# One of three shifted copies of each VectorE score group made on GpSimd, in two forms, in a fused attention and token-MLP kernel

## The chip, the cores and the metric

The kernel runs on one core of a Trainium2 chip. The metric is device time in microseconds, the median of its runs. The profile shows five engines: PE (TensorE), ACT (ScalarE), DVE (VectorE), POOL (GpSimd) and SP (SyncE, which here issues the DMAs). Each works through its own queue in order, and they wait for one another by semaphores.

## What is computed

Cut to what matters (x is 2048 rows of 640 bf16 values, 32 heads of 20, and F = 1536):

```python
xn = layernorm(x)
qkv = xn @ wqkv                                   # 640 x 1920
scores = einsum("bhqd,bhkd->bhqk", q, k) * 20**-0.5
o = einsum("bhqk,bhkd->bhqd", softmax(scores), v)
s = o.transpose(0, 2, 1, 3).reshape(B, S, D) @ wo
u = gelu(einsum("bsd,sf->bdf", layernorm(xn), w1) + b1)
y = einsum("bdf,fs->bds", u, w2) + b2
out = x + s * silu(y.transpose(0, 2, 1))
```

## The kernel before

**Tiles.** Heads are taken four at a time (a group G, with the heads g = 0 to 3 in four 32-row strips of TensorE), queries 512 at a time (p). A pair (G, p) is a pass, 32 in all. In a pass, keys come in 16 chunks of 128, so a pass has 64 score tiles of 128 keys by 512 queries, each made by one matmul (`emit_st`, L1206) into one of the eight PSUM banks.

**Two ways to an exponential.** Most score tiles are exponentiated on ScalarE (`emit_exp`, L1235), two or three banks at a time, into `pt_sb`. The others go to VectorE in groups of four, the four heads of one chunk, called a quad below. VectorE makes the exponential by the bits of bf16: the scores are already scaled so that one unit is 1/128 of a power of two, and adding a constant and storing the sum as an unsigned 16-bit integer gives the bits of a rough exponential. `emit_op1` (L1246) does that straight from PSUM: one instruction a tile, called an eviction below. To smooth the error of the rough curve, `emit_top` (L1268) then makes three copies of the whole quad (2048 elements a partition), shifted by 32, 64 and 96 (`DK`). TensorE multiplies all four versions with `v`, the shifted ones with copies of `v` that are scaled accordingly (`vs_sb`, factors `AK`), and sums them in one PSUM bank (`pv_mm`, L1284). ScalarE's tiles need one such matmul, VectorE's four. Chunks that may go to VectorE are those in `RC`, five of sixteen in a pass.

**Buffers.** `dt_sb` has eight tiles (`NTILE`) of one quad version each; a free list `tfree` hands them out. A quad takes one tile for its evictions and one for each copy, and gives them back when TensorE has read them. At most three quads live at once (`NLIVE`). The two groups of three banks that ScalarE works from (`ACT_GROUPS`) alternate; the last bank of a group can be lent to VectorE (`lent`), and a further bank (`JB`) is shared with the projection and MLP work. A bank whose tile VectorE has evicted is given to the next score matmul, which waits for that eviction.

**What sets the order.** The program is written by a planner that runs when the kernel is built. `Prog` keeps a clock for each engine; every task has a booked cost; `ready` gives the earliest start by the tasks that it depends on. The loop at the end of `schedule` picks the engine that can start first and the candidate of lowest priority number. `pe_cands` and `eng_cands` list the candidates, `OPTS` and `PLAN` change the planner's options every 16 score tiles (`WIN`), and `loads` and `dve_load` estimate what work is left. The finished order stands in the engines' queues; at run time it is fixed, and only semaphores delay it. The rest of the work (projections, MLP matmuls, their evictions and products, the softmax denominators in `ep_steps` with L1400 to L1411, the output) is cut into steps that the planner fits between the score tiles.

**Around the change.** After the fourth eviction of a quad, `emit_op1` puts it on `dtop`. `emit_top` makes copies k = 1, 2, 3 in turn, each a task of VectorE booked at `dv(2048, .26)`. `d["fin"][k]` holds the planned end of version k, which the PV candidate in `pe_cands` uses; versions are multiplied in order of k, some early and the rest later (`PARTS`). With k = 3 the quad leaves `dtop`. GpSimd does small things only: constants and memsets in the lead-in (L503 to L513), the powers of the layer norms (L545, L566), the memset of `wqk_sb` (L1565) and two residual additions in the tail (L1609).

Of the kernel before, what the change touches and what calls it, by code (L numbers as in the profile page):

```python
# [6 lines left out]
dt = mybir.dt  # L7
ALU = mybir.AluOpType
# [31 lines left out]
class Prog:  # L40
# [7 lines left out]
    def __init__(self, nc, n_lanes=8):  # L48
        self.nc = nc
        self.n_lanes = n_lanes  # L50
        self.cengs = list(self.COMPUTE) + [f"d{i}" for i in range(n_lanes)]
        self.cidx_of = {c: i for i, c in enumerate(self.cengs)}
        self.tasks = {e: [] for e in self.COMPUTE}
        self.ctasks = {c: [] for c in self.cengs}
        self.gcount = 0
        self.lane_rr = 0
        self.known = {e: [0] * len(self.cengs) for e in self.COMPUTE}
        self.T = {e: 0.0 for e in self.COMPUTE}
        self.busy = {e: 0.0 for e in self.COMPUTE}
        self.pipe = 0.0  # L60
        self.pe_end = 0.0
        self.low = 0
        self.lowt = 0.0
        self.alog = []

    def lat(self, eng, src):
        return 0.0 if src == eng else self.LAT[eng] + (40.0 if eng == "act" and src == "pe" else 45.0 if eng == "dve" and src == "pe" else 0.0)
# [15 lines left out]
                    r = max(r, t.fin + self.lat(eng, t.ceng))  # L83
        return r

    def _add(self, eng, ceng, fn, reads, writes, name, extra_req=(), cost=100.0, tail=None):
        t = _Task(eng, ceng, fn, name)
        t.gidx = self.gcount
        self.gcount += 1
        self.tasks[eng].append(t)  # L90
        self.ctasks[ceng].append(t)
        t.cidx = len(self.ctasks[ceng])
        req = {}

        def need(tt):
            if tt is None:
                return
            if eng == "pe" and tt.ceng == "pe":
                return
            cur = req.get(tt.ceng)  # L100
            if cur is None or tt.cidx > cur.cidx:
                req[tt.ceng] = tt

        for s in reads:
            assert s.w is not None, f"read of uninit slot {s.name} by {name}"
            need(s.w)
        for s in writes:
            need(s.w)
            for r in s.readers.values():
                if r is not t:  # L110
                    need(r)
        for tt in extra_req:
            need(tt)
        start = self.T[eng]
        for tt in req.values():
            start = max(start, tt.fin + self.lat(eng, tt.ceng))
        kn = list(self.known[eng])
        for tt in sorted(req.values(), key=lambda x: -x.gidx):
            ci = self.cidx_of[tt.ceng]
            if kn[ci] >= tt.cidx:  # L120
                continue
            t.waits[tt.ceng] = tt
            if tt.ceng in self.COMPUTE:
                tt.need_inc = True
            klg = tt.klg
            for i in range(len(kn)):
                if klg[i] > kn[i]:
                    kn[i] = klg[i]
        self.known[eng] = list(kn)
        kn[self.cidx_of[ceng]] = max(kn[self.cidx_of[ceng]], t.cidx)  # L130
        t.klg = kn
        for s in reads:
            s.readers[ceng] = t
        for s in writes:
            s.w = t
            s.readers = {}
        t.t0 = start
        if ceng not in self.COMPUTE:
            start = max(start, 700.0)
            if tail is not None:  # L140
                self.T[eng] = start + cost
                self.pipe = max(self.pipe, start) + cost
                t.fin = self.pipe - cost + tail
            else:
                self.T[eng] = start + 450.0
                self.pipe = max(self.pipe, start + 600.0) + cost
# [27 lines left out]
    def dve(self, fn, reads=(), writes=(), name="dve", cost=300.0):  # L174
        return self._add("dve", "dve", fn, reads, writes, name, cost=cost)

    def pool(self, fn, reads=(), writes=(), name="pool", cost=500.0):
        return self._add("pool", "pool", fn, reads, writes, name, cost=cost)
# [82 lines left out]
class _Kern:  # L261
# [75 lines left out]
        "00000100100010", "10020100100010", "30000100100010", "00002000001000", "01012000000000", "00000000000000",  # L337
        "00000320000000", "00022310000000", "00022311000000",
    )
    PARTS = (2,)  # L340
    DX = (1, 2, 3)
    V1A, V1B = 0.8, 4.0
# [15 lines left out]
    def build(self):  # L358
# [4 lines left out]
        with es:  # L363
# [30 lines left out]
            sb("b1h_sb", [P, FC], f32)  # L394
            sb("b2h_sb", [P, NB], f32)
            sb("bload_sb", [P, FC + NB], bf)
            t["ps_all"] = E(nc.psum_tensor("ps_all", [P, 4096], f32))
            t["qk_dram"] = nc.dram_tensor("qk_scratch_dram", [2, 560, S], bf)
            t["oT_dram"] = nc.dram_tensor("oT_scratch_dram", [8 * P, S], bf)
# [16 lines left out]
    def schedule(self):  # L416
# [80 lines left out]
        def small(fn):  # L497
            def f(e):
# [5 lines left out]
        pr.pool(lambda e: e.memset(cst_sb[:, 1:2], 1.0), writes=[S_("csc")], name="csc0", cost=60)  # L504
        pr.pool(lambda e: e.memset(cst_sb[0:64, 1:2], self.LOG2E * 128.0 / math.sqrt(float(DH))), reads=[S_("csc")],
                writes=[S_("csc")], name="csc1", cost=60)
        pr.pool(lambda e: e.memset(idb_sb[:], 0.0), writes=[S_("idb")], name="id0", cost=200)
        pr.pool(lambda e: e.affine_select(idb_sb[:], idb_sb[:], pattern=[[-1, P]], compare_op=ALU.not_equal, fill=1.0,
                                          base=0, channel_multiplier=1), reads=[S_("idb")], writes=[S_("idb")],
# [551 lines left out]
        dop1 = []  # L1061
        lent = set()
        dtop = []
        pv_pass = [0]
        pv_tot = [UP] * NP
        pv_left = [UP]
# [103 lines left out]
        def d_take(g, bk):  # L1170
            d = d_cur[0]
            if d is None:
                q, c, r = d_claimable()
                claimed.add((q, c))
                dlive[0] += 1
                d = d_cur[0] = dict(q=q, c=c, r=r, todo=[0, 1, 2, 3], tl=[tfree.pop(0), None, None, None], fin=[0.0] * 4, left=4, pk=0)
# [12 lines left out]
            return u  # L1189
# [52 lines left out]
        def emit_op1():  # L1242
            d, g, bk = dop1.pop(0)
            w = dt_sb[:, d["tl"][0], g, :]
            src = ps(bk)
            tk = pr.dve(lambda e: e.tensor_scalar(w, src, WOFF, 0.0, ALU.add, ALU.max), reads=[bank_slot[bk]],  # L1246
                   writes=[S_(f"dt{d['tl'][0]}_{g}")], name=f"dw{d['q']}_{d['c']}_{g}", cost=601.0)
# [12 lines left out]

        def emit_top():
# [5 lines left out]
            dk = float(self.DK[k])  # L1267
            tk = pr.dve(lambda e: e.tensor_scalar(dst, src, dk, None, ALU.add),  # L1268
                        reads=[S_(f"dt{b0}_{g}") for g in range(4)], writes=[S_(f"dt{b}_{g}") for g in range(4)],
                        name=f"dT{d['q']}_{d['c']}_{k}", cost=dv(2048, .26))  # L1270
            dtop[0][1] += 1
            d["fin"][k] = tk.fin
            if k == 3:
                dtop.pop(0)
                if not self.EARLY:
                    dquads.append((tk.fin, d))
                if d["pk"] > 0:
                    tfree.append(b0)

        def pv_mm(q, g, lhsT, rhs, reads, cost, name, last):  # L1280
            k = pv_seen.get((q, g), 0)
# [31 lines left out]
        def emit_pv(items, quads):  # L1313
# [6 lines left out]
            for d, n_ in quads:  # L1320
                for k in range(d["pk"], d["pk"] + n_):
                    for g in range(4):
                        seq.append(("d", d, k, g))
                    if k > 0 or d["tl"][3] is not None:
# [340 lines left out]
        def pe_cands(T):  # L1665
# [27 lines left out]
            if acc_ok[0] and pv_pass[0] < NP:  # L1693
# [28 lines left out]
                okp = bool(pick) and (min(cnt) >= 1 or len(pick) == rem or (tail and len(mine)))  # L1722
                if quads:
                    d0 = quads[0][1]
                    have = sum(f > 0.0 for f in d0["fin"])
# [104 lines left out]
        def dve_load(T):  # L1830
            x = max(0.0, pr.T["dve"] - T) + 602.0 * len(dop1)
            for d, k in dtop:
                x += 600.0 * (4 - k)
            return x

        def do_st(grp, us):
# [52 lines left out]
        def eng_cands(eng, T):  # L1889
# [11 lines left out]
            if eng == "dve":  # L1901
# [3 lines left out]
                if dtop and tfree:  # L1905
                    d, k = dtop[0]
                    b0, b = d["tl"][0], tfree[0]
                    c.append((self.TOPP, pr.ready("dve", [S_(f"dt{b0}_{g}") for g in range(4)],
                                             [S_(f"dt{b}_{g}") for g in range(4)]), emit_top))
            return c  # L1910

        def loads():
# [7 lines left out]
            live += [x[0] for x in dop1] + [x[0] for x in dtop]  # L1920
            for x in {id(x): x for x in live}.values():
                pe += 216.0 * (4 - x["pk"])
                d += 597.0 * sum(f == 0.0 for f in x["fin"][1:])
            return a - done_cost["act"], pe - done_cost["pe"], d - done_cost["dve"]

        self.loads = loads
# [85 lines left out]
```

The softmax here doesn't subtract the row's maximum and nothing guards it: scores larger than these inputs give would overflow.

## Time and profile before

| | |
|---|---|
| median of 2 runs | 755.69 us (755.53 to 755.85) |
| profiled execution, span | 753.7 us |
| ACT busy | 729.9 us (97%), 695 instructions |
| DVE busy | 721.0 us (96%), 1320 instructions |
| PE busy | 717.6 us (95%), 10302 instructions |
| POOL busy | 15.6 us (2%), 22 instructions |
| exponentials, L1235 | 672, 710.5 us |
| evictions, L1246 | 496, 328.2 us |
| shifted copies, L1268 | 372, 241.9 us, median 689 ns each |
| granted TensorE clock | 1.000 |

The span runs from the first to the last instruction of one profiled execution; the median of the runs is 2.0 us longer. Busy time counts an engine's own instructions, not what it issues or waits for. Consecutive instructions of an engine overlap a little, so 372 copies of 687 ns on average count 241.9 us. In the groups of instructions, the figures after the bar are busy time, the mean length of one, and the idle time of the engine just before the group with what ended it.

### The profile page before, as it was taken

Reading aid. Unit: us, or ns where it says so; the run is one execution under the profiler, and the core shown is the slowest. Engines: PE = TensorE matmul, PEld = TensorE weight load, DVE = VectorE, ACT = ScalarE, POOL = GpSimd, SP = SyncE. Lnnn points to the kernel's source line nnn. Section 1 sums busy time; section 2 is a strip of 40 time slices with the busy share of each in tenths; the row PEclk is TensorE's granted clock in tenths of the full one; section 3 lists DMA queues with packets and bytes.
Section 4 is the critical chain, followed back from the end, with each engine's and each line's share of the span. In section 5 each row is a group of like instructions: output and inputs, shape, how many; then the busy total and the mean of one; then the engine's idle time right before and its main releaser. Section 6 shows DMA issues by size and latency. Waiting matters only on the chain.

```text
span 753.7 us, 23158 instructions
## 1 busy us (share of the span) xinstructions
PE 717.6 (95%) x10302; PEld 240.7 (32%) x10302; DVE 721.0 (96%) x1320; ACT 729.9 (97%) x695; POOL 15.6 (2%) x22
## 2 busy tenths in 40 slices
PE   9999999999999999999999999999999988998997
PEld 7432223222323232323223323233333232222222
DVE  8869999999999999999999999999999999999997
ACT  4999999999999999999999999999999999999993
POOL 4200000000000000000000000000000000000001
PEclk9999999999999999999999999999999999999999
DMA  9584111110313031121014022223124340011011
GB/s 245 109 167 57 38 26 38 20 36 7 86 14 77 13 68 38 35 61 21 7 37 111 26 49 52 47 54 102 44 57 82 76 150 11 6 47 48 13 47 36
DMA packets 117143, 42.54 MB, mean 56 GB/s; under 512 B 75300, under 2 KB 115876, under 8 KB 116996
## 3 DMA queue, kind: packets, MB, share of 16 engines
q1 hardware_dynamic: 117044, 41.07, 23.9%
q8 instruction: 80, 1.31, 0.7%
q14 instruction: 19, 0.16, 0.1%
HBM read 26.37 MB, written 10.22 MB: 49 GB/s over the span
## 4 chain that ended last, share of the span: by engine, by line
ACT 85%; PE 12%; DVE 2%; DMA 1%; issue 0%; POOL 0%
ACT pt_sb L1235 83%; PE ps_all L1284 4%; PE ps_all L644 4%; PE ps_all L1206 4%; ACT zt_sb L840 1%; ACT zt_sb L835 1%; PE ps_all L929 1%; DMA xnT_sb<-regC 1%; DVE bst_sb L531 0%; DVE bst_sb L533 0%; DMA regA<-in_A_x_dram 0%; DVE regC L549 0%; DVE regC L1607 0%; PE ps_all L683 0%; DVE xnT_sb L611 0%
## 5 line engine op out<-in xcount | busy, mean ns | idle before, releaser
L1235 ACT ACTIVATE pt_sb<-ps_all 128x1024 bf16<-128x1024 f32 (+1 forms) x672 | 710.5, 1226 | 2.4 <-PE ps_all L1206 1.9
L1246 DVE TENSOR_SCALAR dt_sb<-ps_all 128x512 uint16<-128x512 f32 x496 | 328.2, 684 | 10.1 <-PE ps_all L1206 8.3
L1206 PE MATMUL ps_all<-qk_sb 32*128 32x512 bf16 x2048 | 266.7, 384 | 27.7 <-ACT pt_sb L1235 24.8
L1268 DVE TENSOR_SCALAR dt_sb<-dt_sb 128x2048 uint16<-128x2048 uint16 x372 | 241.9, 687 | 1.4
L1206 PEld LDWEIGHTS ps_all<-qk_sb 32*128 32x128 bf16 x2048 | 67.0, 91 | 283.8 <-ACT pt_sb L1235 231.8
L1284 PE MATMUL ps_all<-dt_sb,vs_sb 128*21 128x512 bf16 x1488 | 124.6, 382 | 0.8 <-DVE dt_sb L1268 0.7
L1284 PE MATMUL ps_all<-pt_sb,v_sb 128*21 128x512 bf16 x1552 | 124.2, 382 | 0.9 <-DVE tr_sb L1400 0.6
L644 PE MATMUL ps_all<-regB,regA 128*32 128x128 bf16 (+1 forms) x1536 | 68.2, 301 | 0.7 <-DVE regB L845 0.3
L644 PE MATMUL ps_all<-regC,regA 128*32 128x512 bf16 (+1 forms) x1536 | 68.4, 301 | 0.0
L1284 PE MATMUL ps_all<-dt_sb,v_sb 128*21 128x512 bf16 x496 | 49.0, 384 | 0.3 <-DVE tr_sb L1400 0.2
L644 PE MATMUL ps_all<-xnT_sb,wqk_sb 128*32 128x512 bf16 x640 | 48.2, 382 | 0.3 <-DVE zt_sb L814 0.2
L1284 PEld LDWEIGHTS ps_all<-dt_sb,vs_sb 128*21 128x21 bf16 x1488 | 31.5, 91 | 41.3 <-issue 21.9
L1284 PEld LDWEIGHTS ps_all<-pt_sb,v_sb 128*21 128x21 bf16 x1552 | 28.7, 90 | 47.7 <-issue 38.0
L644 PEld LDWEIGHTS ps_all<-regB,regA 128*32 128x32 bf16 x1536 | 27.2, 96 | 27.0 <-issue 13.1
L644 PEld LDWEIGHTS ps_all<-regC,regA 128*32 128x32 bf16 x1536 | 27.3, 96 | 25.6 <-issue 13.4
L929 PE MATMUL ps_all<-wv_sb,xnT_sb 128*128 128x128 bf16 (+3 forms) x160 | 29.5, 302 | 0.1
L644 PE MATMUL ps_all<-wv_sb,xnT_sb 128*32 128x480 bf16 x320 | 23.0, 369 | 0.0
L1400 DVE STREAM_TRANSPOSE tr_sb<-ps_all 128x512 f32<-128x512 f32 x31 | 22.1, 711 | 0.9 <-PE ps_all L1284 0.7
L644 PEld LDWEIGHTS ps_all<-xnT_sb,wqk_sb 128*32 128x32 bf16 x640 | 13.7, 95 | 18.2 <-issue 7.7
L1284 PEld LDWEIGHTS ps_all<-dt_sb,v_sb 128*21 128x21 bf16 x496 | 12.6, 90 | 21.3 <-issue 14.7
L814 DVE TENSOR_SCALAR zt_sb<-ps_all,b2h_sb 128x512 bf16<-128x512 f32 (+1 forms) x32 | 17.2, 544 | 0.0
L1044 DVE CAST v_sb<-ps_all 128x480 bf16<-128x480 f32 (+1 forms) x22 | 13.4, 610 | 3.3 <-PE ps_all L737 3.1
(82 smaller groups left out, 307.0 us busy)
## 6 DMA issues: line engine op xcount, KB each, us to landing
regA<-in_B_w_dram SPq DMA_DIRECT2D x6, 1024.0 KB
regA<-in_B_w_dram SPq DMA_DIRECT2D x8, 768.0 KB
qk_sb<-qk_scratch_dram SPq DMA_DIRECT2D x56, 80.0 KB
qk_scratch_dram<-qs_sb SPq DMA_DIRECT2D x32, 128.0 KB
regA<-in_A_x_dram SPq DMA_DIRECT2D x6, 640.0 KB
ok_scratch_dram<-on_sb SPq DMA_DIRECT2D x96, 20.0 KB
out_dram<-regC SPq DMA_DIRECT2D x3, 640.0 KB
wqk_sb<-in_A_wqkv_dram SPq DMA_DIRECT2D x2, 480.0 KB
```

What stands on the lines that cost most here:

```text
L644: fns.append(lambda e, c=c, e_=e_: e.matmul(oc(c, e_), lhsT[:, c:e_], rhs, start=start, stop=stop, tile_position=(0, c)))
L814: steps.append(("dve", lambda e, z=z, i=i, jj=jj: e.tensor_scalar(z[:, c0:c0 + n], ps(bk, n, i * n), 0.5, bias[:, jj:jj + 1], ALU.mult, AL ...
L835: steps.append(("act", lambda e: e.activation(tt_, tt_, AF.Tanh, scale=1.5957691216), [stt], [stt], f"th{j}", ac(n)))
L840: steps.append(("act", lambda e: e.activation(tt_, z, AF.Tanh), sz, [stt], f"th2_{j}", ac(n)))
L929: steps.append(("pe", lambda e, c=c, k=k: e.matmul(ap, oT_sb[0:k, c, b * 128:(b + 1) * 128], wo_ap[0:k, c, c0:c0 + n], start=(opens and c ...
L1044: return lambda e: e.tensor_copy(dst, src)
L1206: pr.pe(lambda e, outp=outp, lhsT=lhsT, rhs=rhs, g=g: e.matmul(outp, lhsT, rhs, start=True, stop=True, tile_position=(32 * g, 0)), reads=[ ...
L1235: tk = pr.act(lambda e: e.activation(outp, inp, AF.Exp, scale=math.log(2.0) / 128.0), reads=[bank_slot[b] for b in banks[:n]], writes=[S_( ...
L1246: tk = pr.dve(lambda e: e.tensor_scalar(w, src, WOFF, 0.0, ALU.add, ALU.max), reads=[bank_slot[bk]], writes=[S_(f"dt{d['tl'][0]}_{g}")], n ...
L1268: tk = pr.dve(lambda e: e.tensor_scalar(dst, src, dk, None, ALU.add), reads=[S_(f"dt{b0}_{g}") for g in range(4)], writes=[S_(f"dt{b}_{g}" ...
L1284: pr.pe(lambda e: e.matmul(outp, lhsT, rhs, start=(k == 0), stop=last, tile_position=(0, 32 * g)), reads=reads, writes=[bank_slot[AB]], na ...
L1400: steps.append(("dve", lambda e: e.transpose(tr_sb[:, :], ps(AB)), [bank_slot[AB]], [S_("tr")], f"epT{q}", 632.0))
```

## The change

The third copy (k = 3) of each quad moves from VectorE to GpSimd. Quads are numbered; an even one is made as before, an immediate added to 2048 two-byte integers, and an odd one as 1024 32-bit integers, each of which holds two neighbours, to which a 32-bit constant with 96 in both halves is added (`sh_sb`, broadcast along the row). A quad's GpSimd task may be planned as soon as its four evictions are, independent of the two VectorE copies. The planner books 2000 ns (`GCOST`) for either form. A new clock pair `port` makes the planner place VectorE's copies and GpSimd's additions so that they do not overlap in its plan; it puts no wait into the program and holds for no other operation. The estimates of VectorE's remaining work count two copies a quad in place of three. `PLAN` is as it was.

```diff
+        self.port = {"dve": 0.0, "pool": 0.0}
...
+        if lock:
+            start = max(start, self.port["pool" if eng == "dve" else "dve"])
+            self.port[eng] = start + cost
...
+    GCOST = 2000.0
...
+            sb("sh_sb", [P, 4], dt.int32)
...
+        sh16 = t["sh_sb"][:, 0:1].bitcast(u16)
+        pr.pool(lambda e: e.memset(sh16, float(self.DK[3])), writes=[S_("shc")], name="shc", cost=60)
...
             if d["left"] == 0:
                 dtop.append([d, 1])
+                ptop.append(d)
...
-                        name=f"dT{d['q']}_{d['c']}_{k}", cost=dv(2048, .26))
+                        name=f"dT{d['q']}_{d['c']}_{k}", cost=dv(2048, .26), lock=True)
...
-            if k == 3:
+            if k == 2:
                 dtop.pop(0)
+            issued(d)
...
+        def emit_ptop():
+            d = ptop.pop(0)
+            b0, b = d["tl"][0], tfree.pop(0)
+            d["tl"][3] = b
+            src = dt_sb[:, b0, :, :]
+            dst = dt_sb[:, b, :, :]
+            if d["n"] % 2:
+                i32 = dt.int32
+                s32 = bass.AP(dt_sb, b0 * 2048, [[self.NTILE * 2048, P], [1, 2048]]).bitcast(i32)
+                d32 = bass.AP(dt_sb, b * 2048, [[self.NTILE * 2048, P], [1, 2048]]).bitcast(i32)
+                c32 = bass.AP(t["sh_sb"], 0, [[4, P], [0, 1024]])
+                fn = lambda e: e.tensor_tensor(d32, s32, c32, ALU.add)
+            else:
+                dk = float(self.DK[3])
+                fn = lambda e: e.tensor_scalar(dst, src, dk, None, ALU.add)
+            tk = pr.pool(fn, reads=[S_(f"dt{b0}_{g}") for g in range(4)] + [S_("shc")],
+                         writes=[S_(f"dt{b}_{g}") for g in range(4)], name=f"dP{d['q']}_{d['c']}_3", cost=self.GCOST,
+                         lock=True)
+            d["fin"][3] = tk.fin
+            issued(d)
...
+            if eng == "pool" and ptop and tfree:
+                b0, b = ptop[0]["tl"][0], tfree[0]
+                c.append((30.0, max(pr.port["dve"], pr.ready("pool", [S_(f"dt{b0}_{g}") for g in range(4)],
+                                                             [S_(f"dt{b}_{g}") for g in range(4)])), emit_ptop))
```

Since the copies of a quad can now end out of turn, `prefix(d)` counts how many versions are done in order of k, and the PV candidate uses that count; `issued(d)` returns the first tile once all three copies have been planned.

More of the change, by code (lines that the diff above doesn't have):

```diff
@@ L84, in ready, with _add @@
         return r
-    def _add(self, eng, ceng, fn, reads, writes, name, extra_req=(), cost=100.0, tail=None):
+    def _add(self, eng, ceng, fn, reads, writes, name, extra_req=(), cost=100.0, tail=None, lock=False):
         t = _Task(eng, ceng, fn, name)
@@ L172, in act, with dve, pool @@
         return self._add("act", "act", fn, reads, writes, name, cost=cost)
[L174 to L178, printed above, removed]
+    def dve(self, fn, reads=(), writes=(), name="dve", cost=300.0, lock=False):
+        return self._add("dve", "dve", fn, reads, writes, name, cost=cost, lock=lock)
+    def pool(self, fn, reads=(), writes=(), name="pool", cost=500.0, lock=False):
+        return self._add("pool", "pool", fn, reads, writes, name, cost=cost, lock=lock)
     def dma(self, fn, reads=(), writes=(), name="dma", lane=None, cost=3000.0, over=(), tail=None):
@@ L1063, in schedule @@
         dtop = []
+        ptop = []
         pv_pass = [0]
@@ L1175, in d_take @@
                 dlive[0] += 1
-                d = d_cur[0] = dict(q=q, c=c, r=r, todo=[0, 1, 2, 3], tl=[tfree.pop(0), None, None, None], fin=[0.0] * 4, left=4, pk=0)
+                d = d_cur[0] = dict(q=q, c=c, r=r, todo=[0, 1, 2, 3], tl=[tfree.pop(0), None, None, None], fin=[0.0] * 4, left=4, pk=0, iss=0, n=stats["dve_units"] // 4)
                 stats["dve_units"] += 4
@@ L1269, in emit_top, with issued, prefix @@
                         reads=[S_(f"dt{b0}_{g}") for g in range(4)], writes=[S_(f"dt{b}_{g}") for g in range(4)],
-                        name=f"dT{d['q']}_{d['c']}_{k}", cost=dv(2048, .26))
+                        name=f"dT{d['q']}_{d['c']}_{k}", cost=dv(2048, .26), lock=True)
             dtop[0][1] += 1
             d["fin"][k] = tk.fin
-            if k == 3:
+            if k == 2:
                 dtop.pop(0)
+            issued(d)
[19 more added lines that the diff above has]
+            issued(d)
+        def issued(d):
+            d["iss"] += 1
+            if d["iss"] == 3:
                 if not self.EARLY:
-                    dquads.append((tk.fin, d))
+                    dquads.append((max(d["fin"]), d))
                 if d["pk"] > 0:
-                    tfree.append(b0)
+                    tfree.append(d["tl"][0])
+        def prefix(d):
+            n = 0
+            while n < 4 and d["fin"][n] > 0.0:
+                n += 1
+            return n
         def pv_mm(q, g, lhsT, rhs, reads, cost, name, last):
@@ L1323, in emit_pv @@
                         seq.append(("d", d, k, g))
-                    if k > 0 or d["tl"][3] is not None:
+                    if k > 0 or d["iss"] == 3:
                         freed.append(d["tl"][k])
@@ L1724, in pe_cands @@
                     d0 = quads[0][1]
-                    have = sum(f > 0.0 for f in d0["fin"])
+                    have = prefix(d0)
                     left = have - d0["pk"]
@@ L1832, in dve_load @@
             for d, k in dtop:
-                x += 600.0 * (4 - k)
+                x += 600.0 * (3 - k)
             return x
@@ L1907, in eng_cands @@
                     b0, b = d["tl"][0], tfree[0]
-                    c.append((self.TOPP, pr.ready("dve", [S_(f"dt{b0}_{g}") for g in range(4)],
-                                             [S_(f"dt{b}_{g}") for g in range(4)]), emit_top))
+                    c.append((self.TOPP, max(pr.port["pool"], pr.ready("dve", [S_(f"dt{b0}_{g}") for g in range(4)],
+                                             [S_(f"dt{b}_{g}") for g in range(4)])), emit_top))
+            if eng == "pool" and ptop and tfree:
+                b0, b = ptop[0]["tl"][0], tfree[0]
+                c.append((30.0, max(pr.port["dve"], pr.ready("pool", [S_(f"dt{b0}_{g}") for g in range(4)],
+                                                             [S_(f"dt{b}_{g}") for g in range(4)])), emit_ptop))
             return c
@@ L1922, in loads @@
                 pe += 216.0 * (4 - x["pk"])
-                d += 597.0 * sum(f == 0.0 for f in x["fin"][1:])
+                d += 597.0 * sum(f == 0.0 for f in x["fin"][1:3])
             return a - done_cost["act"], pe - done_cost["pe"], d - done_cost["dve"]
```

## The prediction

> **What bounds the kernel now.** I read the busy table first, then the cost groups of ScalarE and VectorE, then the busy time by stretch.
>
> ```profile
> span 753.7 us, 23158 instructions
> PE 717.6 (95%) x10302; PEld 240.7 (32%) x10302; DVE 721.0 (96%) x1320; ACT 729.9 (97%) x695; POOL 15.6 (2%) x22
> ```
>
> Three engines stand within 12 us of each other, so the shares alone do not say which one sets the end. The idle time in front of the groups does:
>
> ```profile
> L1235 ACT ACTIVATE pt_sb<-ps_all 128x1024 bf16<-128x1024 f32 (+1 forms) x672 | 710.5, 1226 | 2.4 <-PE ps_all L1206 1.9
> L1246 DVE TENSOR_SCALAR dt_sb<-ps_all 128x512 uint16<-128x512 f32 x496 | 328.2, 684 | 10.1 <-PE ps_all L1206 8.3
> L1206 PE MATMUL ps_all<-qk_sb 32*128 32x512 bf16 x2048 | 266.7, 384 | 27.7 <-ACT pt_sb L1235 24.8
> L1268 DVE TENSOR_SCALAR dt_sb<-dt_sb 128x2048 uint16<-128x2048 uint16 x372 | 241.9, 687 | 1.4
> ```
>
> The 672 exponentials wait 2.4 us in all, while the score matmuls wait 24.8 us for them: ScalarE is the bound, TensorE follows it, and VectorE runs level with it. The stretches show where ScalarE idles at all (columns after the length: PE, PEld, DVE, ACT, POOL busy):
>
> ```profile
> 20.00:40.00 20.00, 17.95 (x188) 7.89 (x188) 16.77 (x59) 20.00 (x16) 4.52 (x4) 1.00 0.64 132
> 40.00:120.00 80.00, 76.36 (x978) 22.98 (x982) 73.56 (x131) 79.18 (x77) 0.00 (x0) 1.00 0.34 60
> ...
> 300.00:400.00 100.00, 97.02 (x1500) 30.61 (x1497) 97.36 (x168) 99.78 (x98) 0.00 (x0) 1.00 0.15 32
> 400.00:500.00 100.00, 96.50 (x1617) 32.22 (x1614) 97.60 (x171) 100.00 (x98) 0.00 (x0) 1.00 0.26 62
> ...
> 740.00:754.00 14.00, 9.92 (x78) 3.60 (x77) 8.06 (x19) 1.76 (x2) 2.26 (x2) 1.00 0.13 47
> ```
>
> From 40 to 740 us ScalarE is busy 698.5 of 700 us. Everything else it idles lies in the lead-in and the tail, which the change hardly touches.
>
> **What it removes.** 124 of the 372 VectorE copies, at 241.9/372 = 0.65 us of busy time each: 80.6 us. VectorE's sum falls from 721.0 to 640.4 us. What stands in the order of the built program decides what this is worth: 672 exponentials before and after, 496 evictions before and after. The planner gives VectorE no more score tiles, so ScalarE keeps its 729.9 us, and the freed VectorE time can buy back at most the 2.4 us ahead of the exponentials. I take -1 us.
>
> **What it adds, and its price.** 124 GpSimd additions, alternately 2048 two-byte elements with an immediate and 1024 words with a tensor of constants. The trace has neither; its rows of GpSimd bound both:
>
> ```profile
> L1609 POOL TENSOR_TENSOR regC<-regC,regA 128x512 bf16<-128x512 bf16 x2 | 2.3, 1148 | 237.8 <-DVE regC L1607 237.8
> ...
> L511 POOL MEMSET wp_sb<- 128x1280 bf16 x1 | 1.2, 1164 | 0.0
> ...
> L508 POOL TENSOR_SCALAR_AFFINE_SELECT idb_sb<-idb_sb 128x128 bf16<-128x128 bf16 x1 | 0.3, 292 | 0.2 <-POOL idb_sb L507 0.2
> ...
> L1633 POOL MEMSET idb_sb<- 128x128 bf16 x1 | 0.2, 204 | 0.0
> ```
>
> The two memsets give (1164-204)/1152 = 0.83 ns an element over a fixed 0.10 us. The two-input addition is (1148-97)/512 = 2.05 ns an element; the select, with one input and an index pattern, (292-97)/128 = 1.5 ns. The packed form is that two-input addition on 1024 words: 0.10 + 2.10 = 2.2 us (a pure write of 1024 elements would give 0.95 us). The two-byte form lies between a memset's 1.8 us and the select's 3.2 us; since it has the read but no pattern, I take 2.0 us, near the memset. The planner itself books 2.0 us for either, and its bookings for the rows above (1200 and 1180 ns) are close to them. GpSimd's sum is then 62 x 2.0 + 62 x 2.2 = 260 us; GpSimd itself is no bound. Only the 32-bit form's constant row is read besides; its one small memset at the start costs about 0.1 us under the loads.
>
> The Trainium skill's page "GPSIMD Engine Reference", section 3.1, puts two-input work at about 2.5 cycles an element and the best simple loop at 1.8 cycles, at 1.2 GHz: by that an estimate of 2.1 us for the packed form, as the row says, but 3.1 us for the two-byte one, which would lead to the slow rival's sum below instead of mine.
>
> **The wait it adds.** Whether a VectorE copy can run beside a GpSimd instruction is seen once in the lead-in, as a hint:
>
> ```profile
> 2.75 2.83 POOL L513 MEMSET v_sb<- 128x1024 bf16 x1
> ```
> ```profile
> 5.30 0.31 DVE L542 TENSOR_SCALAR st_sb<-st_sb 128x2 f32<-128x2 f32 x1
> ...
> 6.91 0.17 DVE L542 TENSOR_SCALAR st_sb<-st_sb 128x2 f32<-128x2 f32 x1
> ```
>
> A tiny SBUF-to-SBUF operation that started under the memset took 0.31 us in place of 0.17 and ended at 5.61, just after the memset at 5.58. So I count a VectorE SBUF-to-SBUF operation as standing still until GpSimd's instruction ends, and the reverse. The lower bound is no blocking at all.
>
> The Trainium skill says the same as a rule and against this change ("SBUF — State Buffer", section "Who interferes with whom"): VectorE's fast two-port modes and GpSimd hold one port pair by an exclusive lock, for the whole instruction. By the rule every overlapping copy waits to the end; by the single row alone the size of the effect on a 2048-element copy stays open.
>
> Now the order. In 56 of the 124 quads a VectorE copy directly follows the fourth eviction, so VectorE goes first and GpSimd waits 0.65 us. I then walked VectorE's order from the point where the GpSimd addition can start to the next SBUF-to-SBUF operation, adding the rows' durations; what the addition outlasts this cover by is blocking, if VectorE never idles. Its median is about 1.9 us, mostly three evictions. Summed over 124: 37 us for additions of 1.8 us, 52 for 2.0, 69 for 2.2, 170 for 3.2. At my prices (52+69)/2 = 60 us; with the two-byte form at 3.2 us, (170+69)/2 = 120 us; bounds 0 to 120. VectorE's sum becomes 640.4 + 60 = 700 us, still under 721. So VectorE does not become the bound, but it gets lumpy: behind a blocked copy stand the next evictions (L1246), for which the score matmul that refills that bank waits, two groups later, and behind it the whole TensorE queue and ScalarE.
>
> Of the 60 us, 38 arise at the shifted copies alone, which the planner's new lock already spaces; the other 22 us come from operations that it does not lock (softmax scaling L1411, GELU products, the vs copies). A third of those 22 us should get past the roughly 0.7 us that a bank has in hand: +7 us (0 to 22).
>
> **The third copy is late.** It took 0.65 us right behind two others; now it takes 2.0 to 2.2 us plus up to one VectorE copy in front. For 33 of the 124 the order leaves only one to three ScalarE instructions (1.06 us each: 710.5/672) between its issue and the PV matmul that reads it. Behind that matmul in TensorE's queue stands the next score group. At 0.15 us each: +5 us (0 to 25, the latter where half of them run 1.2 us over).
>
> **The tail.** The last quad's copies were three at 0.65 us; two of them and a GpSimd addition, one behind the other, are 3.4 us: +1.4 us at most. Output-projection matmuls and two later exponentials cover some of it; I take +0.5 (0 to 2.5). SP's and ScalarE's queues keep their instructions, and no DMA is added. GpSimd's own queue now holds the wqk memset (L1565) and the two last additions (L1609) among or behind the copies; nothing else waits for them before the tail, and the memset, which waits for TensorE, stands in the order between two copies, where it can hold back one of them once.
>
> **The sum.** The profiled execution spans 753.7 us; the median of the runs, 755.69, is 2.0 above. 753.7 - 1 + 7 + 5 + 0.5 = 765.2, plus 2.0: 767.2, rounded to 767 us.
>
> **The rivals.**
> *Slower: the two-byte addition runs like the select.* 3.2 us for half of the additions and 120 us of blocking put VectorE at 760 us; with the 13.3 us that it idles in the first 40 and last 14 us that is 774 span, 776 time, and late third copies bring up to 25 us more: 776 to 801, 788 as its middle. For it: the select is the only one-input row. Against: its pattern. It decides once blocking passes 753.7 - 13.3 - 640.4 = 100 us, on the line from 60 at 2.0 us to 120 at 3.2 us: at about 2.8 us for the two-byte form.
> *Hidden.* Blocking is small or falls into VectorE's 80.6 us of new idle time, and PV comes late anyway: 754 to 757. For it: 27.7 us of TensorE waits ahead of the score matmuls. Against: ScalarE has no idle time in which a stall could vanish.
> *Faster by more than 2%*: ScalarE's instructions would have to fall by 15 us, and the order says that they do not. Nearly excluded; 740.
>
> **How the numbers follow.** 2% (740.6 to 770.8) is about what a measurement of this kernel can tell from no change. The forecast (757 to 776) gets 0.45, with 0.10 of it above 770.8; hidden 0.15; the slow rival 0.38, with 0.03 of it below 770.8; faster 0.02. So slower 0.45, within 2% 0.53, faster 0.02. The range runs from the hidden case to the middle of the slow one and somewhat beyond: 755 to 792.
>
> **What would show it.** Right: 672 exponentials at 710 us; idle time ahead of them of 8 to 20 us, put down to score matmuls; the copies' mean above 687 ns by waiting; GpSimd forms near 2.0 and 2.2 us. Wrong: a two-byte form of 2.8 us or more (slow rival), copies that keep 687 ns (hidden), or fewer exponentials.

## The result, and the profile after

The changed kernel takes 1008.64 us (median of 2 runs, 1008.55 to 1008.73) where the kernel before takes 755.69: 1.3345 times as long, with an interval of 1.3306 to 1.3383. Slower by 253 us, far outside the range that was forecast. First the head of its profile:

```profile
span 1006.6 us, 23129 instructions
...
PE 828.6 (82%) x10282; PEld 254.6 (25%) x10282; DVE 861.5 (86%) x1196; ACT 752.0 (75%) x695; POOL 494.1 (49%) x147
```

GpSimd is busy 494 us, not 260 + 16. VectorE, which gave away 124 copies, is busy 140 us longer than before. ScalarE, the bound before, is busy for 75% of the span in place of 97%. The groups say why:

```profile
L1244 ACT ACTIVATE pt_sb<-ps_all 128x1024 bf16<-128x1024 f32 (+1 forms) x672 | 731.3, 1166 | 229.0 <-PE ps_all L1215 220.5
L1301 POOL TENSOR_SCALAR dt_sb<-dt_sb 128x2048 uint16<-128x2048 uint16 x62 | 345.8, 5578 | 282.5 <-DVE dt_sb L1255 275.7
L1255 DVE TENSOR_SCALAR dt_sb<-ps_all 128x512 uint16<-128x512 f32 x496 | 329.0, 681 | 85.9 <-PE ps_all L1215 84.1
L1215 PE MATMUL ps_all<-qk_sb 32*128 32x512 bf16 x2048 | 304.7, 424 | 61.9 <-DVE dt_sb L1255 46.5
L1278 DVE TENSOR_SCALAR dt_sb<-dt_sb 128x2048 uint16<-128x2048 uint16 x248 | 318.6, 1303 | 2.6 <-PE ps_all L1326 1.3
L1298 POOL TENSOR_TENSOR dt_sb<-dt_sb,sh_sb 128x1024 int32<-128x1024 int32 x62 | 132.7, 2141 | 188.6 <-DVE dt_sb L1255 173.9
```

The two-byte addition takes 5.58 us, 2.8 times the forecast; the packed one 2.14, as forecast. VectorE's remaining copies last 1303 ns on average in place of 687, at the same instruction and shape. ScalarE sits idle 229 us ahead of the 672 exponentials, whose number did not change, 220.5 of it for score matmuls; before, it was 2.4. So 227 of the 253 us lie in that number. Most of the rest is busy time of the same exponentials, 731.3 in place of 710.5 us: their mean length fell, but fewer of them follow one another without a pause, and so they overlap less. One piece of the timeline shows the whole chain (start, length in us, engine, line; in brackets the idle time before and its releaser):

```profile
510.70 5.37 POOL L1301 TENSOR_SCALAR dt_sb<-dt_sb 128x2048 uint16<-128x2048 uint16 x1 [3.04 <-DVE dt_sb L1255]
...
512.56 4.05 DVE L1278 TENSOR_SCALAR dt_sb<-dt_sb 128x2048 uint16<-128x2048 uint16 x1
...
516.53 1.27 DVE L1255 TENSOR_SCALAR dt_sb<-ps_all 128x512 uint16<-128x512 f32 x2
517.26 0.60 PE L1215 MATMUL ps_all<-qk_sb 32*128 32x512 bf16 x1 [2.90 <-DVE dt_sb L1255]
...
517.90 1.45 ACT L1244 ACTIVATE pt_sb<-ps_all 128x1536 bf16<-128x1536 f32 x1 [3.07 <-PE ps_all L1215]
```

GpSimd's two-byte addition runs from 510.70 to 516.07. A VectorE copy that is issued at 512.56 ends at 516.61, 0.54 us after GpSimd: it has stood still until GpSimd was done, and most of its usual 0.69 us came after that. The next evictions stand behind it in VectorE's queue and run from 516.53. A score matmul needs the bank that the first of them empties, and has by then held up TensorE for 2.90 us; ScalarE, which needs the scores, sits idle for 3.07. A good part of VectorE's busy time in this profile is therefore time in which it stands blocked: waiting for GpSimd counts as the length of the instruction, not as idle time in front of it. Idle time alone would not have shown this.

### The profile page after: what moved, and what is told of

It reads as the page before. It is cut to its first block, busy times and chain, and to the rows that moved or that the text cites. A ratio compares the mean times of both kernels' runs of the same rounds, so it can differ in the third digit from the quotient of the medians.

```text
span 1006.6 us, 23129 instructions
## 1 busy us (share of the span) xinstructions
PE 828.6 (82%) x10282; PEld 254.6 (25%) x10282; DVE 861.5 (86%) x1196; ACT 752.0 (75%) x695; POOL 494.1 (49%) x147
## 4 chain that ended last, share of the span: by engine, by line
PE 46%; DVE 43%; ACT 7%; issue 2%; DMA 0%; DVEq 0%; SPq 0%
DVE dt_sb L1278 20%; PE ps_all L1326 16%; PE ps_all L1215 15%; PE ps_all L652 13%; DVE dt_sb L1255 11%; ACT pt_sb L1244 7%; PE ps_all L937 2%; DVE on_sb L1453 2%; DVE zt_sb L851 1%; DVE tr_sb L1442 1%; DVE zt_sb L822 1%; DVE regC L962 1%; DVE regC L952 1%; DVE zt_sb L837 1%; DVE qs_sb L1055 1%
## 5 line engine op out<-in xcount | busy, mean ns | idle before, releaser
L1244 ACT ACTIVATE pt_sb<-ps_all 128x1024 bf16<-128x1024 f32 (+1 forms) x672 | 731.3, 1166 | 229.0 <-PE ps_all L1215 220.5
L1301 POOL TENSOR_SCALAR dt_sb<-dt_sb 128x2048 uint16<-128x2048 uint16 x62 | 345.8, 5578 | 282.5 <-DVE dt_sb L1255 275.7
L1215 PE MATMUL ps_all<-qk_sb 32*128 32x512 bf16 x2048 | 304.7, 424 | 61.9 <-DVE dt_sb L1255 46.5
L1278 DVE TENSOR_SCALAR dt_sb<-dt_sb 128x2048 uint16<-128x2048 uint16 x248 | 318.6, 1303 | 2.6 <-PE ps_all L1326 1.3
L1298 POOL TENSOR_TENSOR dt_sb<-dt_sb,sh_sb 128x1024 int32<-128x1024 int32 x62 | 132.7, 2141 | 188.6 <-DVE dt_sb L1255 173.9
L1326 PE MATMUL ps_all<-dt_sb,vs_sb 128*21 128x512 bf16 x1488 | 141.3, 434 | 88.1 <-DVE dt_sb L1278 88.0
L1326 PE MATMUL ps_all<-pt_sb,v_sb 128*21 128x512 bf16 x1552 | 137.1, 419 | 0.7 <-ACT pt_sb L1244 0.2
L652 PE MATMUL ps_all<-regB,regA 128*32 128x128 bf16 (+1 forms) x1536 | 78.2, 335 | 4.6 <-DVE zt_sb L822 4.5
L652 PE MATMUL ps_all<-xnT_sb,wqk_sb 128*32 128x512 bf16 x640 | 55.7, 430 | 4.9 <-DVE dt_sb L1255 3.1
L1453 DVE TENSOR_TENSOR on_sb<-tr_sb,rden_sb 128x320 bf16<-128x320 f32 x31 | 29.7, 959 | 0.2
```

Of the source, the lines that this page charges most:

```text
L652: fns.append(lambda e, c=c, e_=e_: e.matmul(oc(c, e_), lhsT[:, c:e_], rhs, start=start, stop=stop, tile_position=(0, c)))
L1215: pr.pe(lambda e, outp=outp, lhsT=lhsT, rhs=rhs, g=g: e.matmul(outp, lhsT, rhs, start=True, stop=True, tile_position=(32 * g, 0)), reads=[ ...
L1244: tk = pr.act(lambda e: e.activation(outp, inp, AF.Exp, scale=math.log(2.0) / 128.0), reads=[bank_slot[b] for b in banks[:n]], writes=[S_( ...
L1298: fn = lambda e: e.tensor_tensor(d32, s32, c32, ALU.add)
L1301: fn = lambda e: e.tensor_scalar(dst, src, dk, None, ALU.add)
L1326: pr.pe(lambda e: e.matmul(outp, lhsT, rhs, start=(k == 0), stop=last, tile_position=(0, 32 * g)), reads=reads, writes=[bank_slot[AB]], na ...
```

## The experiments

**The price of the forms, and what they block.** This run (one execution) has none of the kernel's work. It issues each GpSimd form three times by itself, and then VectorE operations under a running form, always after one eviction. In outline:

```diff
+ ("ts2048", tensor_scalar(pb[:, 0:2048], pa[:, 0:2048], 96.0, None, add))   # likewise 1024, 512
+ ("tt1024", tensor_tensor(ib[:, 0:1024], ia[:, 0:1024], constant word, add))
+ ("cp2048", tensor_copy), ("tsbf1280", "tsf1024": immediate add, bf16 and f32), ("ms1280", memset), ("pow16", power)
+ for g in (ts2048, tt1024, pow16, ms1280): for k in (copy4, twoin, f32in, evict): g on GpSimd; evict, k on VectorE
```

> The whole computation is left out; GpSimd forms stand alone, three of each, and then VectorE operations are issued under a running GpSimd form. Price theory: the two-byte addition takes about 5.5 us for 2048 elements with no VectorE work at all, and about half and a quarter for 1024 and 512; the packed one 2.2 us for 1024 words. Rival: the two-byte addition is as short alone as forecast, about 2 us, and its 5.5 us in the changed kernel are waiting for VectorE. Under a running form of 5.5 us, by exclusive blocking: the 2048-element copy and the two-input SBUF product last until that form ends (some 4 us), the eviction from PSUM keeps its 0.68 us; without blocking all keep their time. Under a memset the two-input product should run on if only reads are shared.

The forms, as groups (busy us, mean ns of one; a group of seven holds three by themselves and four beside VectorE):

```profile
L311 POOL TENSOR_SCALAR pb_sb<-pa_sb 128x2048 uint16<-128x2048 uint16 x7 | 37.6, 5368 | 17.9 <-DVE sh_sb L352 17.7
...
L314 POOL TENSOR_TENSOR ib_sb<-ia_sb,sh_sb 128x1024 int32<-128x1024 int32 x7 | 13.2, 1891 | 0.2
...
L324 POOL TENSOR_SCALAR fb_sb<-fa_sb 128x1024 f32<-128x1024 f32 x3 | 8.3, 2770 | 0.2
L311 POOL TENSOR_SCALAR pb_sb<-pa_sb 128x1024 uint16<-128x1024 uint16 x3 | 8.3, 2769 | 0.2
...
L321 POOL COPY pb_sb<-pa_sb 128x2048 uint16<-128x2048 uint16 x3 | 5.7, 1894 | 0.1
L311 POOL TENSOR_SCALAR pb_sb<-pa_sb 128x512 uint16<-128x512 uint16 x3 | 4.5, 1489 | 0.2
```

All seven two-byte additions of 2048 elements lie within 0.02 us of one another, so the form takes 5.37 us with no VectorE work beside it, and its length is its own price and not waiting: (5368-1489)/1536 = 2.5 ns for each further element. It is the immediate addition that is slow, not the two-byte type: 1024 elements take 2.77 us in f32 as in uint16, while a plain two-byte copy of 2048 elements takes 1.89 us, and so does the packed addition of 1024 words. Now VectorE's operations, in order of time: the copy and the two-input product under the two-byte addition, the product under the packed addition, the copy under the power, the copy and the product under the memset. Below them stand the three additions:

```profile
98.56 5.13 DVE L335 TENSOR_SCALAR kb_sb<-ka_sb 128x2048 uint16<-128x2048 uint16 x1
...
104.49 3.30 DVE L338 TENSOR_TENSOR ha_sb<-hc_sb,ha_sb 128x640 bf16<-128x640 bf16 x1
...
123.91 1.56 DVE L338 TENSOR_TENSOR ha_sb<-hc_sb,ha_sb 128x640 bf16<-128x640 bf16 x1
...
130.89 0.69 DVE L335 TENSOR_SCALAR kb_sb<-ka_sb 128x2048 uint16<-128x2048 uint16 x1
...
143.47 0.89 DVE L335 TENSOR_SCALAR kb_sb<-ka_sb 128x2048 uint16<-128x2048 uint16 x1
...
145.16 0.48 DVE L338 TENSOR_TENSOR ha_sb<-hc_sb,ha_sb 128x640 bf16<-128x640 bf16 x1
```

```profile
97.77 5.37 POOL L311 TENSOR_SCALAR pb_sb<-pa_sb 128x2048 uint16<-128x2048 uint16 x1
...
103.81 5.37 POOL L311 TENSOR_SCALAR pb_sb<-pa_sb 128x2048 uint16<-128x2048 uint16 x1
...
123.22 1.89 POOL L314 TENSOR_TENSOR ib_sb<-ia_sb,sh_sb 128x1024 int32<-128x1024 int32 x1
```

The copy ends at 103.69, 0.55 us after the addition's end at 103.14: most of its 0.69 us came after that end. Under the packed addition and under a memset it also ends 0.55 us after them; under a power of 16 elements it keeps its 0.69 us. The product, expected to last until the addition's end, took 3.30 us in place of 0.48 under the two-byte addition and ended at 107.79, 1.4 us ahead of the addition's end at 109.18: held up, but not to the end. Under the packed addition it did last to the end and beyond: it ended at 125.47, 0.36 us after it. Under the memset it ran freely. Evictions from PSUM were never held up (two took 1.42 us under the two-byte addition).

**Only one form.** One line decides the form:

```diff
-            if d["n"] % 2:
+            if True:       # all packed      (if False: all two-byte)
```

> All 124 third copies on GpSimd in the packed 32-bit form; the booking of 2.0 us stays. Price theory (the two-byte form at 5.5 us, while it holds VectorE's copies up, makes the loss; the packed form at 2.2 us does not): 756 to 772 us, VectorE copies at 0.70 to 0.85 us on average, blocking of some 70 us in VectorE's busy time. Rival, structure theory (any addition on GpSimd beside VectorE's copies unsettles the fixed order, the form matters little): over 850 us, since half of the loss at least would stay.

> All 124 third copies on GpSimd in the two-byte form; the booking of 2.0 us stays. Price theory: the loss of 253 us about doubles, 1200 to 1350 us, GpSimd busy about 690 us. Structure theory: little more than the changed kernel, 1000 to 1080 us.

All packed: 789.93 us, 1.0455 times before (1.0428 to 1.0483). All two-byte: 1137.35 us (one run), VectorE's copies at 1699 ns. So, in this order, putting the packed form in place of the two-byte one takes away 219 of the 253 us: with 62 of them the kernel goes from 790 to 1009 us, with 124 to 1137. Both expectations missed in size. The second 62 add 129 us, not as much as the first. And the packed form alone is not free: 34 us stay, more than the 16 that the price theory allowed.

**The order without the additions.** The same queues in the same order, with the addition reduced, from the fifth quad on, to a memset of two elements:

```diff
+            if d["n"] >= 4:
+                fn = lambda e: e.memset(t["sh_sb"][:, 2:3].bitcast(u16), 0.0)
...
```

> The changed kernel's order, unchanged in every queue, but from the fifth quad on the addition is a GpSimd memset of two elements (0.1 us), so the third copy is not made and its PV matmul reads an old tile. It holds what the planned order costs with the addition at next to nothing. If the order itself is as good as before's: 752 to 757 us, and all of the 34 us that the packed-only kernel loses come from the 2.1 us additions. If the order, whose option list was not chosen for this work, brings a loss of its own: 765 to 785 us.

768.28 us, ratio 1.0153 (1.0129 to 1.0176). So 12.4 us of the loss are in the order itself, before any addition is paid for. Its groups of exponentials and copies:

```profile
L1244 ACT ACTIVATE pt_sb<-ps_all 128x1024 bf16<-128x1024 f32 (+1 forms) x672 | 714.8, 1196 | 14.0 <-PE ps_all L1215 9.3 <-PE ps_all L1328 3.2
...
L1278 DVE TENSOR_SCALAR dt_sb<-dt_sb 128x2048 uint16<-128x2048 uint16 x248 | 165.3, 685 | 3.0 <-PE ps_all L1328 1.7
```

VectorE is busy 659.6 us here and its copies keep 685 ns. This is the baseline for blocking: 861.5 - 659.6 = 202 us in the changed kernel.

**Blocking or lateness.** Two halves of the mechanism, each alone, in the same order. These are the main lines of two edits; the powers, too, run from the fifth quad on:

```diff
 # blocking alone: PV of the third copy reads a constant tile
-                    rhs = dt_sb[:, b, g, :].bitcast(bf)
+                    rhs = wp_sb[:, 0:2, :, :] if k == 3 else dt_sb[:, b, g, :].bitcast(bf)
...
 # lateness alone: powers of 33 or 12 elements in place of the additions
+                fn = lambda e: e.tensor_tensor(pw[:, 64:64 + n_], pw[:, 0:n_], pw[:, 0:n_], ALU.pow)
```

> The changed kernel's order and its additions as they are, but the PV matmul of the third copy reads a constant tile in its place and so does not wait for GpSimd. Blocking theory (GpSimd stops VectorE's copies and products, and VectorE's evictions behind them stop TensorE): 950 to 1008 us, nearly the whole loss stays. Lateness theory (TensorE waits for the late third copy, with the next score group behind it): under 850 us.

> The changed kernel's order, but from the fifth quad on GpSimd computes powers of 33 or 12 elements in place of the additions, which take about as long (5.5 and 2.3 us by the forms run) and under which VectorE's copies kept their 0.69 us there; the third copy is not made, and its PV matmul waits for GpSimd as before. Blocking theory: 755 to 800 us, VectorE copies at 0.69 us on average. Lateness theory: 900 us or more.

Blocking alone: 1012.12 us (one run), the whole loss, with the same long copies and the same idle time ahead of the exponentials:

```profile
L1244 ACT ACTIVATE pt_sb<-ps_all 128x1024 bf16<-128x1024 f32 (+1 forms) x672 | 731.6, 1167 | 231.5 <-PE ps_all L1215 221.9 <-PE ps_all L1326 6.8 <-PE ps_all L652 0.3
...
L1278 DVE TENSOR_SCALAR dt_sb<-dt_sb 128x2048 uint16<-128x2048 uint16 x248 | 319.8, 1307 | 2.6 <-PE ps_all L1326 1.3
```

PV's wait for GpSimd costs nothing on top. The changed kernel's own trace agrees: among its waits there is none of TensorE for GpSimd, and of VectorE only 1.9 us, in the layer norm. Lateness alone: 813.9 us (one run), 46 us above the order without additions, more than the blocking theory allowed and less than the lateness theory asked. There the copies keep their time, and TensorE waits for GpSimd itself:

```profile
L1280 DVE TENSOR_SCALAR dt_sb<-dt_sb 128x2048 uint16<-128x2048 uint16 x248 | 165.3, 685 | 3.0 <-PE ps_all L1332 1.7
...
L1332 PE MATMUL ps_all<-dt_sb,vs_sb 128*21 128x512 bf16 x1488 | 129.6, 391 | 37.7 <-POOL pw_sb L1298 26.7 <-DVE dt_sb L1280 10.4
```

(The powers ran 5.89 and 2.49 us, a little longer than the additions.) The two do not add up. The likely reading is that VectorE, blocked by the same addition, is as late as the third copy is and hides it; no run tests that by itself.

**Blocking alone, all packed.** The same constant tile in the packed-only kernel:

> The packed-only kernel, whose PV matmul of the third copy reads a constant tile and does not wait for GpSimd; the same order as the run without additions. Of the 21.7 us between that run (768.3) and the packed-only kernel (789.9), blocking theory: all stay, 786 to 790 us. Lateness theory: 768 to 775 us.

788.45 us, ratio 1.0426 (1.0409 to 1.0444), not to be told from the packed-only 1.0455 (1.0428 to 1.0483). So the packed kernel's 34 us are some 12 us of order and some 20 us of blocking (VectorE 695 us busy against 659.6), and PV's wait is within the noise. Of the 35 us by which VectorE is busy longer, 12.8 lie in the copies and the rest in products and other SBUF operations that the planner's lock does not cover.

**What the planner did not know.** The two-byte and the packed form are booked at about what they take:

```diff
-                         writes=[...], name=f"dP{d['q']}_{d['c']}_3", cost=self.GCOST,
+                         writes=[...], name=f"dP{d['q']}_{d['c']}_3", cost=2250.0 if d["n"] % 2 else 5550.0,
```

> The changed kernel with the measured prices booked in the planner (5550 ns for the two-byte form, 2250 ns for the packed one, in place of 2000 for both); the work is the same. If the loss comes from the planner's ignorance of the price (the copies are planned into the time that the addition still takes, and the PV matmuls too early): 760 to 800 us. If it comes from the price itself (GpSimd additions, VectorE copies and VectorE's other SBUF operations need 62 x 5.55 + 62 x 2.25 + 161 + about 66 = 711 us of one shared resource, one at a time): above 850 us still.

845.58 us (one run): between the two expectations, just under the bound for the price and far above the one for ignorance. With the prices booked the planner gives VectorE 107 quads in place of 124 and ScalarE more tiles (745.4 us of exponentials in place of 731.3), and the copies last less long (860 ns). The booking recovers 163 us; with this option list 90 us stay. So nearly two thirds of the loss hung on an order that was made for 2.0 us. How much of the 163 us comes from better placing, and how much from the 17 quads fewer, this run does not tell.

**What the option list is worth, and the best that was tried.** First the kernel before with `PLAN = ()`, then the packed form booked at 2150 ns, the port clock held also for VectorE's other SBUF operations, and a list searched for these bookings:

```diff
+        lock = lock or name.rstrip("0123456789_") in self.PORTED     # epm, vs, GELU and residual operations
...
-    GCOST = 2000.0
+    GCOST = 2150.0
```

> The kernel before without its list of planner options (the defaults throughout); no addition on GpSimd, three copies on VectorE. It shows what an order is worth whose options were not picked for its own tasks. If the 12 us that the order of the changed kernel costs without its additions are such a misfit: 760 to 772 us here too. If the list is worth nothing: 755 to 757 us, and the 12 us have another cause.

> All third copies packed, booked at 2150 ns, with the port clock held also against VectorE's two-input and other SBUF operations, and the list of options searched anew for these bookings (118 quads in place of 124). If the loss of the packed-only kernel is planning: 756 to 770 us. If it is the price of one shared port: 772 to 790 us. Faster than before is not expected, since ScalarE gets no less work.

The kernel before without its list: 763.40 us, ratio 1.0097 (1.0082 to 1.0112). An order with unchosen options (122 quads in it) costs it 7.2 us, so a misfit of the list could make a good part of the 12.4 us above; that it is the same cause was not shown. The packed version with these bookings: 772.86 us, 1.0222 (1.0207 to 1.0238), 17 us better than the packed-only kernel, and still behind the kernel before:

```profile
L1246 ACT ACTIVATE pt_sb<-ps_all 128x1024 bf16<-128x1024 f32 (+1 forms) x674 | 723.0, 1218 | 8.0 <-PE ps_all L1217 6.7 <-PE ps_all L1328 0.2
```

Even with little idle time left (8.0 us), there is nothing to win: ScalarE has no fewer exponentials than before. With 118 quads in place of 124 it takes over 24 score tiles, and its exponentials are busy 723.0 us where they were busy 710.5, which is 12.5 of the 17 us behind the kernel before. No version here beats the kernel before.

**The clock.** TensorE's granted clock fell to 0.877 over the changed run, and its matmuls got longer (score matmuls 384 to 424 ns). To see whether this carries a share of its own, 1488 zero matmuls were put ahead of the PV matmuls that wait for VectorE's copies, in the changed kernel and in the one without additions:

```diff
+                    if g == 0 and k in (1, 2) and all(pv_seen.get((q, z), 0) > 0 for z in range(4)):
+                        ... # 3 - k groups of four zero matmuls into the PV bank
```

> The changed kernel with 1488 more zero matmuls (three groups of four a quad) in TensorE's queue just ahead of the PV matmuls that wait for VectorE's two copies; all else and its order are the same. They give TensorE work while VectorE stands blocked, at 12 x 0.054 = 0.65 us a quad, 80 us in all where nothing is blocked. If the low granted clock (0.877) carries a share of the 253 us: the clock rises above 0.92 and the time falls below 1000 us. If the clock only follows from the stalls and costs nothing of its own: 1010 to 1060 us.

> The same 1488 zero matmuls in the kernel that has the changed order but no additions (768.3 us without them): the price of the filling by itself. TensorE is 94% busy there, so most of their 80 us should show: 810 to 850 us. If they fall into its gaps: under 790 us.

The clock rose to 0.931 and the time stayed, 1010.77 us (ratio 1.3284 to 1.3459). The filling by itself costs 55 us in the kernel without blocking (823.27 against 768.28). So the changed kernel took the filling in without getting slower or faster. Whether it vanished in the stalls, or cost something that the better clock gave back, these runs do not tell. The clock's own share stays open.

## Why the prediction was wrong

**The bound, and no gain.** Right: 672 exponentials and 496 evictions before and after, and ScalarE's idle time is where the loss shows. There was nothing to win, which the runs without additions (768 us) and with honest booking (773 us) are in keeping with.

**The price: the step that failed.** The two-byte addition was put at 2.0 us, with 3.2 as its upper end. It takes 5.37 us alone and 5.58 in the kernel, well past the 2.8 us that the prediction itself named as a sign of being wrong. It was placed between a memset and the affine select, whose 1.5 ns an element made the upper end since it has one input; the two-input addition's 2.05 ns priced only the packed form. None of these rows bounds 2.6 ns. The assumption that failed is that fewer operands make a GpSimd instruction cheaper: with their whole length divided by their elements, the copy, with the same operands and no arithmetic, has 0.92 ns, the packed addition with a second operand 1.85, and the immediate addition 2.6. The argument from the planner's bookings, close to two other rows, did not help, since 2000 was booked for both forms. The packed form's 2.2 us came out (2.14), with some luck: alone it takes 1.89 us, and the rest comes only beside VectorE.

The Trainium skill's page "GPSIMD Engine Reference", section 3.1, gives 1.8 cycles an element for the best simple loop, by which the prediction quoted 3.1 us. The runs show 5.37 us, and 2.5 ns for each further element are 3.0 cycles at that page's 1.2 GHz. The measurement decides; the page's figure would have left the forecast wrong too, though nearer. The 2.5 cycles that the prediction quotes for two-input work stand in that page's section 2.1; section 3.1 has 2.6.

**The blocking: right in mechanism.** The exclusive wait read from one operation of 0.31 us is confirmed on 2048-element copies. Carried on from the prediction's own sums, the walk gives at most about 265 us at 5.55 and 2.2 us (170/2 at 3.2 us, 62 x 2.35 for the rest, and 69/2); 202 us were measured. For the packed form alone it gives 69 us, and 35 us were measured (694.8 - 659.6), so the walk is high, as a bound without VectorE's idle time should be. What was wrong is the baseline: VectorE without additions is busy 659.6 us, not 640.4, since operations with gaps between them overlap less.

**What gets past to ScalarE: also wrong.** A third of 22 us was forecast; the 38 us at the shifted copies were put at nothing, because the planner's lock spaces them. That holds only as far as the booked 2.0 us is true: the copies were blocked for 12.8 us in the packed-only kernel, and in the changed one for 153 of the 202 us (318.6 against 165.3); with the real prices booked, their mean fell from 1303 to 860 ns. The third was too low as well. In the packed-only kernel some 20 us get through of 35 us of blocking; in the changed one the loss over the order without additions is about 240 us, more than the 202 of blocking. So with the price right the sum would still have fallen short: the packed-only kernel, whose 2.12 us are near both assumed prices, takes 790 us, not 767. A short stall may be absorbed in part by the 0.7 us that a bank was said to have in hand, and a long one not; no run measures that, and the clock is lower as well (what that adds stays open).

**The slow rival** had the right mechanism and the right condition, blocking above 100 us, but its price ended at 3.2 us, and so its time at 801.

**The late third copy** was given 5 us, up to 25; alone, behind powers of 5.89 and 2.49 us, it costs 46, beside the blocking nothing that shows.

**The order's own loss** of 12.4 us had no term in the sum at all: the prediction took an order with the same counts for an equally good one.

The Trainium skill's rule in "SBUF — State Buffer", section "Who interferes with whom", by which the later of the two waits for the whole instruction, holds for the copies under the additions and the memset, which end 0.55 us after it, and not under the power, where the copy kept its 0.69 us. For the two-input product it is too strict under the two-byte addition, since the product ended 1.4 us ahead of that; under the packed one it holds. Where the two differ, the measurement decides.

## What to carry to other kernels

SBUF-to-SBUF work like these copies, moved from VectorE to GpSimd, is paid for twice: on GpSimd, and on VectorE by every copy that has to stand still under it, which the profile books as a longer instruction and not as idle time. Price a GpSimd form by a row of that same operation, or leave the upper end open: operand counts and element sizes say little (0.92, 1.85 and 2.6 ns an element for copy, word addition and immediate addition). A planner's lock spaces such work only as well as the price that it is booked at. And ask first whether the engine that is relieved sets the end: here it did not, and the best version tried is still 2% behind.

## What the runs showed of the hardware that was not expected

- GpSimd's addition of an immediate costs 2.6 to 2.7 ns an element in two-byte integers and in f32 alike (2048 two-byte elements 5.37 us, 1024 f32 2.77 us), nearly three times its copy (2048 elements 1.89 us). Two 16-bit additions packed into a 32-bit word addition take 1.89 us for the same 4096 bytes.
- A GpSimd power of 16 elements runs 2.9 us and holds up nothing on VectorE; a memset of 1.17 us holds up a VectorE copy to its end but no two-input product.
- A two-input VectorE product is held up by both GpSimd additions, but not by both to the end: under the two-byte one of 5.37 us it takes 3.30 us in place of 0.48 and is done 1.4 us before it; under the packed one of 1.89 us it takes 1.56 us and ends 0.36 us after it.
